# One routing step, token number times expert one-hot, read from constants in PSUM instead of from the one-hot in SBUF

## The chip, the cores and the metric

The program runs on one core of one Trainium2 chip. The metric is the device time of one execution in microseconds (us), lower is better. The core has five engines with instruction queues of their own: PE (matrix multiply), DVE (VectorE, elementwise and reductions), ACT (ScalarE), POOL (GpSimd) and SP (which issues most DMAs). Engines wait for one another on semaphores only; each runs its own queue strictly in order.

## What is computed

The reference is three layers, one after the other, on 768 tokens:

```python
attn_out = _attn_ref(**attn_kwargs)      # 8 heads, 64 wide, masked by hash bucket
x = attn_out.transpose(0, 2, 1, 3).reshape(B, S, H * D)     # 768 x 512
x = _moe_ref(x=x, **moe_kwargs)          # gMLP: w_in, gelu, spatial gate w_sg, w_out
return _moe2_ref(x=x, **moe2_kwargs)     # sticky top-1 mixture of 8 experts
...
for s in range(S):                       # in _moe2_ref
    fresh_e = int(np.argmax(logits[b, s]))
    e = fresh_e if s == 0 or local_gate[b, s] < 0.5 else prev_e
    prev_e = e
    h = np.maximum(x[b, s] @ w1[e], 0.0)
    out[b, s] = p[e] * (h @ w2[e])       # p: softmax of the logits
```

Every token goes to one expert: the one of its own highest logit, or, where its local gate says so, the one of the token ahead of it.

## The kernel before

The 768 tokens are six tiles of 128 (`t` = 0 to 5), a token to a partition. The program has four stretches: attention, the feed-forward part, mixing (spatial gate, output projection, residual, and the routing of each tile), and the eight experts. Every stretch is an order written out by hand: a text such as `MIXING` lists steps by name, and each engine's queue gets its instructions in the order in which the steps come. Nothing is reordered afterwards, so a step that waits holds all that stands behind it on its engine.

Weights of the experts stream in beside all this: step `wr` reads a quarter of a matrix (512 KB) into one of six raw buffers, `wh` casts it on ACT into the high half (L655), and `wl` subtracts the high half to get the low half, on DVE or POOL (L661). The low half is a 128 x 1024 subtraction with both sources in SBUF, and on POOL it runs for over 2 us.

In mixing, PE has four kinds of work, interleaved: `mix` (tile `vs`, L744, spatial gate), `out` (tile `o`, L767, output projection), small transposes and matmuls of the routing, and `gx` (L910, which gathers the tokens of an expert by a matmul with a selection matrix). DVE serves them: `gated` (tile `g`, L748) multiplies a finished `vs`, and PE transposes the product (`gT`, L754); `gl` (L759) splits it; `res` (L770) adds the residual.

The routing of one tile is the generator `route(t)`, and each word `route t` in `MIXING` runs it on to its next `yield`. Its steps are a chain through nearly all engines: transposes of x on PE (L781), logits on PE (tile `lg`, L791 to L799), the maximum on DVE (L802), the choice as a key per token (L819), a transpose of the key on PE into `route_bank` (L822), the running maximum over tokens (L824 to L839), which settles the expert of each token as a number `f` (L844), its one-hot `oh` (L846), ranks within the expert (L854), the selection matrix `pick` (L861), and the two parts of a small table, token number per expert (L868) and probability per expert (L872). The key of the next tile needs `carry` of this one.

`route_bank` is one bank of PSUM. Beside the transposed keys and the exponentials it holds two constants that were copied there once: `rev_p` (L924, eight numbers, one for each expert) and `iota_p` (L925). So L842, L846, L861 and L864 already read their tensor from PSUM. L868 is different: it reads `oh`, which L846 left in SBUF, multiplies by the token number `tok_1` (a scalar per partition) and writes eight numbers per token to `what_all` in SBUF.

Of the kernel before, what the change touches and what calls it, by code (L numbers as in the profile page):

```python
# [15 lines left out]
ALU = mybir.AluOpType  # L16
# [173 lines left out]
def kernel(  # L190
# [15 lines left out]
    nc = tc.nc  # L206
# [21 lines left out]
    tok_1 = sm[:, 32:38]  # L228
# [388 lines left out]
    what_all = cpool.tile([P, NT, 2, NE], F32, name="what_all")  # L617
# [49 lines left out]
    with ExitStack() as ctx_b:  # L667
# [109 lines left out]
        def route(t):  # L777
# [54 lines left out]
            f = bp2.tile([P, 1], F32, tag="rf", name="rf")  # L832
# [8 lines left out]
            oh = oh_all[:, t, :]  # L841
# [23 lines left out]
            yield "slot"  # L865
            nc.vector.tensor_scalar_add(se, se, 1e-9)
            yield "se"
            nc.vector.tensor_scalar(what_all[:, t, 0, :], oh, tok_1[:, t:t + 1], None, op0=ALU.mult)  # L868
            yield "id"
            nc.vector.reciprocal(se, se)  # L870
            yield "rse"
# [51 lines left out]
        rev_p, iota_p = route_bank[:, P:P + NE], route_bank[:, 2 * P:4 * P]  # L923
        nc.vector.tensor_copy(rev_p, revc)  # L924
        nc.scalar.copy(iota_p, iota2)  # L925
        routes = [route(t) for t in range(NT)]

        def side_b(name, t, k=0):
# [167 lines left out]
    with tc.If(n_extra > 0):  # L1096
        with ExitStack() as ctx_x:
# [13 lines left out]
            for t in range(NT):  # L1111
# [6 lines left out]
                                        op0=ALU.is_lt, op1=ALU.mult)  # L1118
                nc.vector.tensor_tensor(at[:, 0:1], at[:, 0:1], at[:, 1:2], op=ALU.add)
                nc.vector.scalar_tensor_tensor(ati, rank_all[:, t:t + 1], -float(P), at[:, 0:1],  # L1120
                                               op0=ALU.add, op1=ALU.add)
# [121 lines left out]
```

## Time and profile before

| | |
|---|---|
| median of 3 runs | 346.63 us (345.64 to 347.73) |
| the profiled execution | 347.04 us |
| its span, first to last instruction | 344.6 us |
| PE busy | 327.5 us (95%) |
| DVE busy | 272.5 us (79%) |
| ACT busy | 233.9 us (68%) |
| POOL busy | 203.5 us (59%) |
| mean granted PE clock | 0.989 of full speed |

Some 2.4 us of the profiled execution lie outside its span. Times within the trace are counted in us from the start of the span. A busy share says how full an engine was on average, not that it set the end: for that, the waits of each stretch and the chain of work that ended last are read. The ends of PE's instructions are modelled, because matmuls overlap in its pipeline; the starts are firmer.

### The profile page before, as it was taken

What the parts mean: (1) busy time and instruction counts of PE and PEld (TensorE: products, weight loads), DVE (VectorE), ACT (ScalarE), POOL (GpSimd) and SP (SyncE); (2) the same over time, 40 slices, a digit from 0 to 9 for tenths busy, and PEclk for the clock granted to TensorE, in tenths of its full rate; (3) what the DMA queues carried; (4) which work ended last, traced back from release to release, by engine and by line L of the source; (5) the groups of instructions that cost most, each with busy time, mean ns of one, the idle gap of its engine ahead of it and who ended that gap; (6) DMA issues with size and microseconds to landing.
All of it is one profiled execution on the core that took longest, in us unless ns stands there. A gap on an engine that the chain in (4) does not pass through costs nothing.

```text
span 344.6 us, 5450 instructions
## 1 busy us (share of the span) xinstructions
PE 327.5 (95%) x1860; PEld 256.8 (75%) x1860; DVE 272.5 (79%) x516; ACT 233.9 (68%) x432; POOL 203.5 (59%) x162
## 2 busy tenths in 40 slices
PE   7899999999999999999989999879999999999992
PEld 6787777667777657788767776559888888788892
DVE  4899999989998865788753768988589868798933
ACT  3589888888888775299455364364659786869540
POOL 3378867688858645247434674865732674574651
PEclk9999999999999999999999999998999999999997
DMA  6914043213421024011107429292979979999510
GB/s 248 331 45 153 3 152 121 92 38 119 133 82 61 10 62 132 0 57 52 46 7 253 124 89 327 81 357 66 343 252 303 336 288 368 348 330 364 216 60 32
DMA packets 25951, 55.82 MB, mean 162 GB/s; under 512 B 2878, under 2 KB 7486, under 8 KB 25920
## 3 DMA queue, kind: packets, MB, share of 16 engines
q1 hardware_dynamic: 23872, 50.67, 42.7%
q0 software_dynamic: 1120, 3.15, 2.7%
q10 hardware_dynamic: 928, 1.62, 1.4%
q8 instruction: 16, 0.26, 0.3%
q14 instruction: 15, 0.12, 0.1%
HBM read 52.28 MB, written 3.67 MB: 162 GB/s over the span
## 4 chain that ended last, share of the span: by engine, by line
PE 73%; DVE 13%; DMA 4%; ACT 4%; issue 2%; POOL 2%; SPq 0%; ACTq 0%; DVEq 0%; POOLq 0%
PE y L1045 10%; PE eh L1013 9%; PE t L437 9%; PE po L453 8%; PE s L420 5%; PE h L314 5%; PE s L423 5%; PE vs L744 5%; DMA raw<-in_w 3%; PE hv L314 3%; PE o L767 3%; PE pj L404 3%; PE gx L910 2%; PE hT L1024 1%; DVE what_all L868 1%
## 5 line engine op out<-in xcount | busy, mean ns | idle before, releaser
L661 POOL TENSOR_TENSOR w<-raw,w 128x1024 fp32r<-128x1024 f32 x23 | 58.6, 2549 | 40.3 <-ACT w L655 40.3
L655 ACT CAST w<-raw 128x1024 fp32r<-128x1024 f32 x64 | 65.3, 1052 | 12.7 <-DMA raw<-in_w 6.0
L661 DVE TENSOR_TENSOR w<-raw,w 128x1024 fp32r<-128x1024 f32 x41 | 59.9, 1492 | 5.1 <-ACT w L655 4.9
L443 ACT COPY pt<-t 128x384 f32<-128x384 f32 x96 | 43.4, 484 | 12.6 <-PE t L437 12.5
L431 ACT ACTIVATE e<-s,nb_all 128x768 f32<-128x768 f32 x48 | 43.6, 909 | 9.7 <-DVE nb_all L427 9.7
L427 DVE TENSOR_REDUCE nb_all<-s 128x1 f32<-128x768 f32 x48 | 45.4, 952 | 5.9 <-PE s L423 5.4
L437 PE MATMUL t<-ident,e 128*128 128x128 f32 x288 | 42.4, 274 | 0.0
L437 PEld LDWEIGHTS t<-ident,e 128*128 128x128 f32 x288 | 34.3, 140 | 8.6 <-ACT e L431 2.4
L453 PE MATMUL po<-pt,vt 128*64 128x384 f32 x192 | 35.4, 497 | 0.0
L1045 PE MATMUL y<-w,hh 128*128 128x512 f32 (+1 forms) x144 | 34.7, 374 | 0.3 <-ACT hh L1030 0.3
L420 PE MATMUL s<-k,q 128*128 128x384 f32 x96 | 28.5, 377 | 0.8 <-ACT e L431 0.7
L1045 PEld LDWEIGHTS y<-w,hh 128*128 128x128 f32 x144 | 24.4, 189 | 4.7 <-ACT hh L1030 0.8
L744 PE MATMUL vs<-vn,wshi 128*128 128x512 f32 x72 | 25.8, 406 | 1.4 <-ACT wshi L735 1.2
L423 PE MATMUL s<-k,q 76*128 76x384 f32 x96 | 25.1, 342 | 0.3 <-DVE q L411 0.3
L1013 PE MATMUL eh<-w,xh 128*128 128x512 f32 x96 | 25.0, 394 | 0.0
L392 POOL TENSOR_TENSOR k<-r,k 64x768 fp32r<-64x768 f32 x7 | 13.8, 1974 | 14.9 <-DVE k L382 9.5
L453 PEld LDWEIGHTS po<-pt,vt 128*64 128x64 f32 x192 | 12.0, 136 | 13.7 <-issue 13.4
L314 PE MATMUL h<-w_in_s,xTs 128*128 128x512 f32 x96 | 21.9, 389 | 0.0
L314 PEld LDWEIGHTS h<-w_in_s,xTs 128*128 128x128 f32 x96 | 18.0, 188 | 3.7
L1013 PEld LDWEIGHTS eh<-w,xh 128*128 128x128 f32 x96 | 17.7, 188 | 3.6
L420 PEld LDWEIGHTS s<-k,q 128*128 128x128 f32 x96 | 14.7, 190 | 7.2 <-ACT e L431 2.5
L1057 POOL DMA_INDIRECT out<-y,dst_row x8 | 12.3, 1532 | 11.2 <-ACT y L1054 4.7
(201 smaller groups left out, 738.4 us busy)
## 6 DMA issues: line engine op xcount, KB each, us to landing
raw<-in_w SPq DMA_DIRECT2D x64, 512.0 KB, 5.2
r<-in_qk SPq DMA_DIRECT2D x7, 768.0 KB, 4.4
raw<-in_w_in SPq DMA_DIRECT2D x8, 512.0 KB, 5.9
wsr<-in_w_sgT SPq DMA_DIRECT2D x6, 384.0 KB, 3.5
raw<-in_w_out SPq DMA_DIRECT2D x4, 512.0 KB, 3.5
vt<-in_v_tok ACTq DMA_DIRECT2D x1, 1536.0 KB, 9.3
xd<-x SPq DMA_DIRECT2D x6, 256.0 KB, 4.4
r<-in_qk SPq DMA_DIRECT2D x2, 384.0 KB, 4.0
```

The costliest lines, as they stand in the source:

```text
L314: nc.tensor.matmul(ps, a[:, kc, ts_], w_in_s[:, b, kc, ns], start=(kc == 0 and i == 0), stop=(kc == 3 and i == 2))
L420: nc.tensor.matmul(s[:, j, :HALF], q1[:, ts_], k1[:, j * HALF:(j + 1) * HALF], start=True, stop=False)
L427: nc.vector.tensor_reduce(nb_all[:, h, t:t + 1], ss[h, t][:, :, :HALF], axis=AX.XY, op=ALU.max, negate=True)
L431: nc.scalar.activation(e, ss.pop((h, t))[:, :, :HALF], AF.Exp, bias=nb_all[:, h, t:t + 1], accum_out=rs_all[:, h, t:t + 1])
L437: nc.tensor.transpose(ps[:, i * P:(i + 1) * P], es[h, t][:, g, i * P:(i + 1) * P], ident)
L443: nc.scalar.copy(dst, tps.pop((h, t, g))[:, :HALF].rearrange("p (i q) -> p i q", i=3))
L453: nc.tensor.matmul(po[j * D:(j + 1) * D, :HALF], vt[:, kt, h * D:(h + 1) * D], pt[j][:, kt, :], start=(kt == 0), stop=(kt == NT - 1))
L655: nc.scalar.copy(slabs_of[i, e][:, 0, q * 2:(q + 1) * 2, :], raws[part])
L661: eng.tensor_tensor(hl[:, 1, q * 2:(q + 1) * 2, :], raws.pop(part), hl[:, 0, q * 2:(q + 1) * 2, :].bitcast(F32), op=ALU.subtract)
L744: nc.tensor.matmul(ps, a[:, kc, :], b[:, kc, :], start=(k == 0), stop=(k == 17))
L1013: nc.tensor.matmul(ps[e, n], a[:, kc, :], slabs_of[1, e][:, b, kc * 2 + n, :], start=(k == 0), stop=(k == 11))
L1045: nc.tensor.matmul(yb[e][:, cs], a[:, kc, :], slabs_of[2, e][:, b, kc, cs], start=(k == 0), stop=(k == 23))
```

## The change

One instruction per tile is formed from other inputs. The one-hot is one where `rev_p` equals `f`; so the product of one-hot and token number can be formed in a single instruction from `rev_p` in PSUM and the two per-partition scalars `f` and `tok_1`, without reading `oh`:

```diff
@@ -865,7 +865,7 @@
             yield "slot"
             nc.vector.tensor_scalar_add(se, se, 1e-9)
             yield "se"
-            nc.vector.tensor_scalar(what_all[:, t, 0, :], oh, tok_1[:, t:t + 1], None, op0=ALU.mult)
+            nc.vector.tensor_scalar(what_all[:, t, 0, :], rev_p, f, tok_1[:, t:t + 1], op0=ALU.is_equal, op1=ALU.mult)
             yield "id"
             nc.vector.reciprocal(se, se)
             yield "rse"
```

The one-hot `oh` is still computed at L846, since L854 and L872 read it. On every engine the same instructions stand in the same places, with the same semaphores to wait for. This is DVE's queue around the step of tile 1, in mixing; `rf` is the scalar `f`, `sm` holds `tok_1`, and `se` is the sum of the softmax:

```order
 L864 TENSOR_SCALAR gbc<-route_bank,rank_all 128x128
 L866 TENSOR_SCALAR se<-se 128x1
-L868 TENSOR_SCALAR what_all<-oh_all,sm 128x8
+L868 TENSOR_SCALAR what_all<-route_bank,rf,sm 128x8
 L748 SCALAR_TENSOR_TENSOR g<-vs_2237,bsg,u_2_2030 128x512
 L759 SCALAR_TENSOR_TENSOR gl<-gT_2334,gh 128x512
```

Only the operands of the one instruction differ; the product `g` for PE's next transposes still stands right behind it. The other five places read alike.

## Rows read from the trace of the kernel before

**Rows 1.** The page's part 4, the chain that ended last, by line.

```profile
PE y L1045 10%; PE eh L1013 9%; PE t L437 9%; PE po L453 8%; PE s L420 5%; PE h L314 5%; PE s L423 5%; PE vs L744 5%; DMA raw<-in_w 3%; PE hv L314 3%; PE o L767 3%; PE pj L404 3%; PE gx L910 2%; PE hT L1024 1%; DVE what_all L868 1%
```

**Rows 2.** By stretch: us; busy PE, PEld, DVE, ACT, POOL; PEclk, DMA share, GB/s.

```profile
204.00:231.00 27.00, 22.45 (x150) 16.90 (x149) 23.36 (x93) 13.12 (x26) 17.85 (x9) 1.00 0.68 233
231.00:235.00 4.00, 3.98 (x20) 3.69 (x21) 2.48 (x14) 1.29 (x3) 4.00 (x4) 0.57 0.35 138
240.00:330.00 90.00, 89.67 (x442) 74.01 (x440) 75.27 (x70) 68.22 (x88) 50.66 (x24) 1.00 0.87 303
```

**Rows 3.** DVE's instructions by line: ns min/median/max, first and last start.

```profile
L868 DVE TENSOR_SCALAR what_all<-oh_all,sm x6: 221/1076/1906, 196.7 to 237.8; 128x8 f32<-128x8 f32 x6
...
L846 DVE TENSOR_SCALAR oh_all<-route_bank,rf x6: 216/226/227, 193.7 to 236.0; 128x8 f32<-128x8 f32 x6
...
L842 DVE TENSOR_SCALAR ohb_all<-route_bank,rf,pm x6: 276/277/285, 193.2 to 235.4; 128x8 bf16<-128x8 f32 x6
```

**Rows 4.** DVE's timeline: start, us, instruction, [idle before it <- releaser].

```profile
196.69 0.89 DVE L868 TENSOR_SCALAR what_all<-oh_all,sm 128x8 f32<-128x8 f32 x1
199.03 0.75 DVE L748 SCALAR_TENSOR_TENSOR g<-vs,bsg,u 128x512 f32<-128x512 f32 x1 [1.45 <-PE vs L744]
...
205.39 0.23 DVE L846 TENSOR_SCALAR oh_all<-route_bank,rf 128x8 f32<-128x8 f32 x1
...
207.03 1.91 DVE L868 TENSOR_SCALAR what_all<-oh_all,sm 128x8 f32<-128x8 f32 x1
...
217.85 1.56 DVE L868 TENSOR_SCALAR what_all<-oh_all,sm 128x8 f32<-128x8 f32 x1
...
219.92 0.15 DVE L802 TENSOR_REDUCE rmx<-lg 128x1 f32<-128x8 f32 x1
...
225.99 1.27 DVE L868 TENSOR_SCALAR what_all<-oh_all,sm 128x8 f32<-128x8 f32 x1
```

**Rows 5.** POOL's timeline, the four subtractions that L868 met.

```profile
195.14 2.40 POOL L661 TENSOR_TENSOR w<-raw,w 128x1024 fp32r<-128x1024 f32 x1
...
204.17 4.74 POOL L661 TENSOR_TENSOR w<-raw,w 128x1024 fp32r<-128x1024 f32 x2 [1.14 <-ACT w L655]
...
216.99 2.39 POOL L661 TENSOR_TENSOR w<-raw,w 128x1024 fp32r<-128x1024 f32 x1
...
224.86 2.37 POOL L661 TENSOR_TENSOR w<-raw,w 128x1024 fp32r<-128x1024 f32 x1 [1.90 <-ACT w L655]
```

**Rows 6.** PE's timeline around its three long waits for DVE.

```profile
207.02 0.39 PE L744 MATMUL vs<-vn,wslo 128*128 128x512 f32 x1
...
208.39 0.50 PE L744 MATMUL vs<-vn,wslo 128*128 128x512 f32 x1
209.65 0.66 PE L754 MATMUL gT<-ident,g 128*128 128x128 f32 x4 [0.76 <-DVE g L748]
...
218.47 0.29 PE L795 MATMUL lg<-cst,lts 128*128 128x9 f32 x2
...
219.40 0.63 PE L767 MATMUL o<-w_out_s,gh 128*128 128x512 f32 x2
221.49 0.29 PE L822 MATMUL route_bank<-ident,key 128*128 128x128 f32 x1 [1.47 <-DVE key L819]
...
228.74 0.30 PE L822 MATMUL route_bank<-ident,key 128*128 128x128 f32 x1 [1.57 <-DVE key L819]
```

**Rows 7.** PE's gx matmuls with x2h: busy us, mean ns; at 225:228, then 231:235.

```profile
L910 PE MATMUL gx<-pick,x2h 128*128 128x256 f32 x4 | 1.1, 299 | 0.0
...
L910 PE MATMUL gx<-pick,x2h 128*128 128x256 f32 x9 | 3.6, 405 | 0.0
```

**Rows 8.** Expert-weight subtractions by line: ns min/median/max, on DVE and on POOL.

```profile
L661 DVE TENSOR_TENSOR w<-raw,w x41: 1207/1218/3420, 181.4 to 328.8; 128x1024 fp32r<-128x1024 f32 x41
...
L661 POOL TENSOR_TENSOR w<-raw,w x23: 2370/2402/3347, 185.8 to 330.8; 128x1024 fp32r<-128x1024 f32 x23
```

## The prediction, made before the changed kernel ran

> **What bounds the kernel now.** I read the chain of work that ended last first. It is PE nearly throughout, but one line of DVE stands in it with 1% of the span: L868, the very instruction that is changed [rows 1]. An instruction of eight elements per partition has no business there, so the next view is its group by line: six executions, from 221 ns to 1,906 ns, with a median of 1,076 ns [rows 3]. Its sister L846, of the same size and also writing to SBUF, but reading from PSUM, never leaves 216 to 227 ns [rows 3]. Two of the six L868 ran in about 0.22 us; the other four took 0.89, 1.91, 1.56 and 1.27 us [rows 4].
>
> What stretches those four is seen by laying POOL's timeline beside DVE's. Each was issued while POOL ran a weight subtraction, and each ended just behind POOL's end: 197.58 against 197.54, 208.94 against 208.91, 219.41 against 219.38, 227.26 against 227.23 [rows 4, 5]. So the long duration is not work. L868, which reads and writes SBUF, is held until POOL is through. An instruction that reads its tensor from PSUM is not: L846 at 205.39 ran in 0.23 us in the middle of POOL's 204.17 to 208.91 [rows 4, 5].
>
> Then, who is late because of it? In 204 to 231 PE was busy for 22.45 of 27 us, so 4.55 us of PE stood empty there [rows 2]. In 240 to 330, the experts, it was busy for 89.67 of 90 us [rows 2]. Before and after this stretch PE has next to nothing to give; here it has, and its three long waits are all for DVE: 0.76 us for `g`, 1.47 and 1.57 us for a key [rows 6]. Each comes a little after one of the long L868 at 207.03, 217.85 and 225.99 [rows 4].
>
> **The change, part by part.** Nothing is added, removed or moved, on any queue; six instructions change one operand from SBUF to PSUM and get a second scalar.
>
> *Price of the new L868.* It is L846 with one more operation and one more scalar. L846 bounds it below (0.216 us); L842, which also reads `rev_p` and two scalars but writes another type, above (0.285 us) [rows 3]. I take 0.22 us, as L846 is nearer in output type. At the upper end, the three on the path would cost 0.2 us in all.
>
> One rule of the Trainium skill speaks against the change ("VectorE: DVE Perf Modes", in its section on the TRN2 errata): a Vector instruction pays a fixed 120 cycles with a source in PSUM against 58 with one in SBUF, at 0.96 GHz. By it, my estimate is some 0.065 us more for each instruction, 0.4 us for the six, and the change would lose wherever POOL is quiet. The rows do not bear this out at eight elements: 0.226 us from PSUM at the median against 0.221 us from SBUF when not held [rows 3]. So the sum goes without it.
>
> *Tile 0, L868 at 196.69.* It would be 0.67 us shorter. But DVE then sat idle for 1.45 us until PE had finished `vs` [rows 4]. That wait covers it: worth nothing, also if the cover shrank by half.
>
> *Tile 1, L868 at 207.03.* 1.91 becomes 0.22 us, and DVE is 1.69 us ahead. The next instruction, `g`, needs the `vs` whose last matmul runs on PE from 207.02 to 207.41 [rows 6], so it starts at about 207.45 and is still early enough. PE waited for it until 209.65, having been through with its last matmul at 208.89 by the modelled end, or free for the next one by about 208.7 by the pace of starts. So PE gains 0.76 to 0.95 us [rows 6]; I take 0.9. PE itself is late next.
>
> *Tile 2, L868 at 217.85.* 1.56 becomes 0.22 us, 1.34 us on DVE. The next maximum, at 219.92, needs the logits that PE finishes at 218.76 [rows 4, 6]; with 0.03 us for the semaphore it can come forward by 1.13 us at most. From there to the key all is in line on DVE and ACT, and PE's wait of 1.47 us is long enough to take all of that [rows 6]. Worth 1.13 us; 0.3 us of wait stay.
>
> *Tile 3, L868 at 225.99.* 1.27 becomes 0.22 us, 1.05 us on DVE. The logits behind it are there, the exponential follows the maximum, and PE's wait of 1.57 us for the key covers it [rows 6]. Worth 1.05 us; 0.5 us of wait stay.
>
> *Tiles 4 and 5.* Not held, 0.22 us before and after [rows 3]: nothing.
>
> *Sum:* 0.9 + 1.13 + 1.05 = 3.1 us by which PE, and all that it releases, reaches the experts earlier. The experts then run as a block: the weights come over buffers that are freed by the same engines, so they start earlier with it. DMA at 0.87 of its time in 240 to 330 is busy but not full [rows 2], and the time behind it is the same. On the profiled execution, 347.04 - 3.1 = 343.9 us. The median of the runs lies 0.41 us below that execution, which makes 343.5 us.
>
> *PE's clock, unknown.* In 231 to 235 the granted clock is 0.57 on average, so PE spent most of it at 1.2 GHz, the lower of its two levels; ahead of that, it had stood waiting for the key [rows 2, 6]. The nine `gx` matmuls with a high half there took 405 ns against 299 ns just before [rows 7]: 9 x 0.106 = 0.95 us, and as much again for those with the low half, which come one for one, 1.9 us in all. With shorter waits PE may keep 2.4 GHz. The bounds are 0 (it falls as before) and 1.9 us; if it does not fall I take 1.0, about the middle, since DVE's chain for tile 5, whose key PE transposes in that stretch, then becomes the bound for the rest. If it falls at another place, a stretch of the same length would cost about the same. In the sum I leave it as it was.
>
> **The rivals.** "Faster" and "slower" mean by more than 0.5%, 1.7 us; within that a measurement of this kernel can't tell it from no change.
>
> *B, the clock holds too.* As forecast, plus 1.0 us: 342.5. For it: the waits ahead of the fall shrink from 1.57 to 0.5 us and from 1.47 to 0.3 us. Against it: some 1.4 of the 4.55 us of idle time stay in the stretch ahead of it.
>
> *C, given back in the experts.* PE comes 3.1 us early, and the weight stream does not: a cast that waits for its DMA holds what stands behind it on ACT, and PE with it. For it: DMA raw stands in the chain with 3% [rows 1], some 10 us. Against it: the reads are released by subtractions that come earlier too. If half or more is lost, 345.0 to 346.6; I put it at 345.6.
>
> *D, the change doesn't do what it says.* L868 is still held, because it also writes to SBUF and reads its scalars there. L846 does both and is not held [rows 3, 4]. Time: 346.6. The Trainium skill ("SBUF — State Buffer", on the two sides of SBUF) has the shared port pair locked by a Vector instruction in a two-port mode or with two SBUF inputs, and held for a whole instruction. By that rule the scalars don't count and D falls; the four ends behind POOL's agree.
>
> *E, slower: the holds come back at L661.* DVE's own subtractions are held by POOL as well: 1,218 ns at the median, 3,420 ns at worst, so a hit costs up to 2.2 us [rows 8]. With DVE 3 us early against POOL the meetings fall anew in the experts, and DVE's queue holds the low halves that PE waits for. Two more hits on the path eat the gain and leave 346.63 - 3.1 + 4.4 = 347.9, within the bound; it decides from three on, 350.1 us. Against it: the meetings of today are as random, and PE stood idle there for only 0.33 us in 90 [rows 2].
>
> **How the numbers follow.** Forecast (A) 0.46: the holds are plain in the rows, and each wait that shrinks is named. B 0.30. C 0.13. D 0.05. E 0.06. A and B are faster: 0.76. C and D are the same: 0.18. E is slower: 0.06. The predicted time is A's, 343.5 us. The range reaches down past B to 341.4 (nearly the full 1.9 us for the clock, and a little scatter of the runs), and up to 345.6, which takes in a loss of two thirds of the gain; most of C, D and E stay outside, together some 0.2.
>
> **What would show it.** All six L868 at about 0.22 us, whatever POOL does. PE's wait for `g` gone, and those for the two keys down to 0.3 and 0.5 us; so PE's idle time in the stretch that was 204 to 231 falls from 4.55 to about 1.4 us. The first expert matmul comes 3.1 us earlier (4.1 in B, with no stretch at half clock). The forecast is wrong if L868 still ends with POOL's L661, if PE meets waits for other work at these places, or if PE's idle time in the experts grows from 0.3 us by as much as was won.

## The result, and the profile after

The changed kernel took 342.85 us, the median of 6 runs (342.15 to 343.22); the kernel before took 346.48 us, the median of 6 (345.55 to 347.73). The ratio is 0.9894, with a 95% interval of 0.9871 to 0.9918: 3.6 us, about 1.1%, faster. The profiled execution has a span of 340.8 us in place of 344.6.

The group of L868 by line in the profile after (ns min/median/max), beside [rows 3]:

```profile
L868 DVE TENSOR_SCALAR what_all<-route_bank,rf,sm x6: 275/276/279, 196.7 to 234.3; 128x8 f32<-128x8 f32 x6
```

The spread of 221 to 1,906 ns is gone. DVE's timeline after, beside [rows 4]:

```profile
207.06 0.28 DVE L868 TENSOR_SCALAR what_all<-route_bank,rf,sm 128x8 f32<-128x8 f32 x1
207.49 0.75 DVE L748 SCALAR_TENSOR_TENSOR g<-vs,bsg,u 128x512 f32<-128x512 f32 x1 [0.15 <-PE vs L744]
...
216.91 0.28 DVE L868 TENSOR_SCALAR what_all<-route_bank,rf,sm 128x8 f32<-128x8 f32 x1
217.87 0.17 DVE L802 TENSOR_REDUCE rmx<-lg 128x1 f32<-128x8 f32 x1
...
223.94 0.28 DVE L868 TENSOR_SCALAR what_all<-route_bank,rf,sm 128x8 f32<-128x8 f32 x1
```

POOL's timeline after, its subtractions at the same places, beside [rows 5]:

```profile
204.19 4.75 POOL L661 TENSOR_TENSOR w<-raw,w 128x1024 fp32r<-128x1024 f32 x2 [1.14 <-ACT w L655]
...
216.05 2.40 POOL L661 TENSOR_TENSOR w<-raw,w 128x1024 fp32r<-128x1024 f32 x1
...
222.82 2.37 POOL L661 TENSOR_TENSOR w<-raw,w 128x1024 fp32r<-128x1024 f32 x1 [0.79 <-ACT w L655]
```

POOL is as busy there as it was (17.89 us against 17.85), and all three L868 run in the middle of its subtractions, in 0.28 us. It is the meeting that became harmless; it didn't move away. PE's timeline after, at the three places of [rows 6], and its first expert matmul:

```profile
208.77 0.60 PE L754 MATMUL gT<-ident,g 128*128 128x128 f32 x4
...
219.45 0.29 PE L822 MATMUL route_bank<-ident,key 128*128 128x128 f32 x1 [0.35 <-DVE key L819]
...
225.71 0.29 PE L822 MATMUL route_bank<-ident,key 128*128 128x128 f32 x1 [0.59 <-DVE key L819]
...
235.51 3.83 PE L1013 MATMUL eh<-w,gxhi 128*128 128x512 f32 x16
```

The wait of 0.76 us is gone, and those of 1.47 and 1.57 us are 0.35 and 0.59 us. Busy time by stretch after, with the columns of [rows 2]:

```profile
204.00:228.00 24.00, 22.31 (x150) 16.98 (x149) 19.70 (x94) 13.15 (x26) 17.89 (x9) 1.00 0.72 244
...
228.00:231.00 3.00, 2.63 (x20) 2.23 (x20) 2.04 (x12) 1.30 (x3) 3.00 (x4) 1.00 0.84 330
231.00:235.00 4.00, 3.69 (x34) 3.31 (x33) 3.68 (x23) 1.39 (x3) 1.90 (x1) 1.00 0.24 31
...
236.00:326.00 90.00, 89.85 (x441) 74.31 (x440) 75.30 (x75) 68.87 (x89) 50.30 (x24) 1.00 0.86 304
```

The same 150 matmuls, in 24 us where they had 27, leave PE idle for 1.69 us, where it was 4.55. The granted clock stays at 1.00 in all these stretches; the half-speed stretch of [rows 2] is not there. And in 90 us of experts PE is idle for 0.15 us: nothing was given back.

### The profile page after: what moved, and what is told of

It reads as the page before. It is cut to its first block, busy times and chain, and to the rows that moved or that the text cites. A ratio compares the mean times of both kernels' runs of the same rounds, so it can differ in the third digit from the quotient of the medians.

```text
span 340.8 us, 5450 instructions
## 1 busy us (share of the span) xinstructions
PE 325.9 (96%) x1860; PEld 255.5 (75%) x1860; DVE 268.1 (79%) x516; ACT 234.4 (69%) x432; POOL 203.4 (60%) x162
## 4 chain that ended last, share of the span: by engine, by line
PE 74%; DVE 11%; ACT 5%; DMA 4%; issue 3%; POOL 2%; SPq 0%; ACTq 0%; POOLq 0%; DVEq 0%
PE eh L1013 9%; PE y L1045 9%; PE t L437 9%; PE po L453 9%; PE vs L744 6%; PE s L420 5%; PE h L314 5%; PE s L423 5%; PE o L767 4%; DMA raw<-in_w 3%; PE hv L314 3%; PE pj L404 3%; PE hT L1024 1%; DMA r<-in_qk 1%; ACT w L655 1%
```

## Experiments

All runs are compared with the kernel before. The executions scatter by some 2 us, so a second measure is read from each profile: the distance from the start of tile 0's L868, up to which nothing changes, to the start of the first expert matmul. In the kernel before it is 42.27 us (196.69 to 238.96), after 38.80 us. What follows the first expert matmul took 105.2 to 105.6 us in every profile.

| kernel | median us | ratio (95% interval) | distance us |
|---|---|---|---|
| the change | 342.85 | 0.9894 (0.9871 to 0.9918) | 38.80 |
| constants in SBUF | 346.22 | 0.9999 (0.9983 to 1.0014) | 42.41 |
| two tensors in SBUF | 346.81 | 1.0013 (0.9998 to 1.0027) | 42.22 |
| tiles 0, 4, 5 only | 346.60 | 1.0012 (0.9996 to 1.0028) | 42.83 |
| tile 1 only | 345.35 | 0.9974 (0.9959 to 0.9988) | 41.33 |
| tile 2 only | 345.40 | 0.9972 (0.9957 to 0.9987) | 41.06 |
| tile 3 only | 345.15 | 0.9958 (0.9941 to 0.9975) | 41.15 |
| all but tile 3 | 344.80 | 0.9947 (0.9923 to 0.9971) | 40.77 |
| before, PE's wait filled | 346.29 | 1.0006 (0.9989 to 1.0023) | 42.08 |
| the same, tile 4 in the new form | 345.84 | 0.9983 (0.9966 to 1.0001) | 42.26 |
| key first | 342.97 | 0.9901 (0.9872 to 0.9931) | 38.48 |
| key first, probability later | 342.08 | 0.9866 (0.9841 to 0.9891) | 37.65 |

The distances are of one execution each, and PE's clock differs among them, as told below.

**What holds L868?** The change does two things at once: the tensor comes from PSUM, and the one-hot is no longer needed. The first run keeps the new form and takes the constants from SBUF:

```diff
-nc.vector.tensor_scalar(what_all[:, t, 0, :], rev_p, f, tok_1[:, t:t + 1], op0=ALU.is_equal, op1=ALU.mult)
+nc.vector.tensor_scalar(what_all[:, t, 0, :], revc, f, tok_1[:, t:t + 1], op0=ALU.is_equal, op1=ALU.mult)
```

> The changed instruction as it is (is-equal to f, times the token number), but the eight constants are read from their copy in SBUF instead of PSUM. Theory (what counts is that the tensor lies in SBUF, and POOL holds such an instruction): L868 of tiles 0 to 3 ends with POOL's subtraction again, 0.9, 1.9, 1.5 and 1.2 us, the first expert matmul starts at about 239.0 us as before, time 346.5. Rival (the gain comes from the new form, which doesn't need the one-hot): 0.28 us each, first expert matmul at 235.5, time 342.9.

DVE's timeline of that run:

```profile
207.03 1.91 DVE L868 TENSOR_SCALAR what_all<-sm,rf 128x8 f32<-128x8 f32 x1
...
235.90 0.28 DVE L868 TENSOR_SCALAR what_all<-sm,rf 128x8 f32<-128x8 f32 x1
```

POOL's timeline of that run:

```profile
204.16 4.75 POOL L661 TENSOR_TENSOR w<-raw,w 128x1024 fp32r<-128x1024 f32 x2 [1.14 <-ACT w L655]
```

Held as before, to 208.94, with POOL through at 208.91, and nothing is gained in time (0.9999). For this instruction the form does nothing, the place of the tensor does all. The traces show no wait for POOL ahead of L868; it starts, and ends late. The opening says that engines wait for one another on semaphores only: this hold is an exception to it.

The unheld 0.28 us at tile 4 also prices the two parts of the new L868: with its tensor in SBUF it takes as long as with it in PSUM (0.276 us), and 0.06 us more than with one scalar. The new form has a second operation, too, but that is not what costs, as an instruction of the same size in the kernel before shows, with two operations and constants in place of both scalars:

```profile
L890 DVE TENSOR_SCALAR none<-table 128x8 f32<-128x8 f32 x1 | 0.2, 156 | 0.0
```

It reads PSUM and takes 0.156 us, against 0.226 us with one scalar and one operation (L846) and 0.277 us with two of each (L842). So it is each scalar read per partition that costs, some 0.06 us, and neither the operation nor PSUM.

The second run is the old product written with two tensors:

```diff
-nc.vector.tensor_scalar(what_all[:, t, 0, :], oh, tok_1[:, t:t + 1], None, op0=ALU.mult)
+nc.vector.tensor_tensor(what_all[:, t, 0, :], oh, tok_1[:, t:t + 1].to_broadcast([P, NE]), op=ALU.mult)
```

> L868 as a product of two tensors in SBUF, the one-hot and the token number broadcast over eight elements, in place of tensor times scalar. Theory (an instruction with two SBUF tensors is held by a POOL instruction that reads SBUF, too): four long ones as before, time 346.5. Rival (only an instruction of one SBUF source is held, since only that can use both read ports for it): about 0.23 us each, first expert matmul at 235.5, time 342.9.

DVE's timeline of that run, and POOL's one subtraction at tile 4:

```profile
206.94 1.90 DVE L868 TENSOR_TENSOR what_all<-oh_all,sm 128x8 f32<-128x8 f32 x1
...
235.44 0.44 DVE L868 TENSOR_TENSOR what_all<-oh_all,sm 128x8 f32<-128x8 f32 x1
237.60 0.16 DVE L868 TENSOR_TENSOR what_all<-oh_all,sm 128x8 f32<-128x8 f32 x1
...
233.50 2.37 POOL L661 TENSOR_TENSOR w<-raw,w 128x1024 fp32r<-128x1024 f32 x1
```

An instruction with two tensors in SBUF is held just as one with a single tensor is; at tile 4, where POOL ends at 235.87, it ends at 235.88. Left alone it takes 0.16 us. Its rival falls. The Trainium skill ("SBUF — State Buffer", on the two sides of SBUF) names two kinds of Vector instruction that meet POOL's lock, one in a two-port mode and one with two SBUF inputs. The holds seen here agree with it, though no trace tells in which mode an instruction ran.

Not every DVE instruction with its tensor in SBUF is held, though. Two others of the kernel before, L866 with one element per partition and L828 with a maximum over 128, and POOL's subtraction beside the second (the one beside the first is in [rows 5]):

```profile
206.97 0.14 DVE L866 TENSOR_SCALAR se<-se 128x1 f32<-128x1 f32 x1
...
213.55 0.29 DVE L828 TENSOR_REDUCE pm<-km 128x1 f32<-128x128 f32 x1
...
213.38 2.40 POOL L661 TENSOR_TENSOR w<-raw,w 128x1024 fp32r<-128x1024 f32 x1 [4.48 <-ACT w L655]
```

Both read and write SBUF, and both ran at once, in the middle of a subtraction. What sets them apart from L868 was not tested.

**Which tiles count?** The new form by a condition on `t`, the old form elsewhere:

```diff
+if t in (0, 4, 5):
     nc.vector.tensor_scalar(what_all[:, t, 0, :], rev_p, f, tok_1[:, t:t + 1], op0=ALU.is_equal, op1=ALU.mult)
+else:
+    nc.vector.tensor_scalar(what_all[:, t, 0, :], oh, tok_1[:, t:t + 1], None, op0=ALU.mult)
```

> The new form for tiles 0, 4 and 5 only. Theory: tile 0's hold is covered by DVE's wait for vs and tiles 4 and 5 are not held, so nothing: first expert matmul at 239.0, time 346.5 within 0.3. Rival (a hold of 0.67 us counts wherever it is): 0.6 us earlier.

Tile 0's L868 fell from 0.89 to 0.28 us and no time was won. The distance is even 0.56 us longer; in this execution the clock was at 0.50 in 231 to 235 and still at 0.84 in 235 to 239, where it was 0.57 and 1.00 before. In the next three runs the condition is `t in (1,)`, `(2,)` and `(3,)`:

> The new form for tile 1 only. Theory: PE's wait for g goes (0.76 us by the modelled ends, 0.9 by the starts), the two waits for keys stay at 1.5 and 1.6 us, the clock falls as before; first expert matmul at 238.1, time 345.6. Rival (the wait is paid at the next place, since DVE has its own chain): 346.5.

> The new form for tile 2 only. Theory: PE's first wait for a key falls from 1.47 to 0.3 or 0.4 us; the maximum behind it waits for the logits, so 1.1 of 1.3 us count; first expert matmul at 237.9, time 345.4. Rival: all of 1.3 us.

> The new form for tile 3 only. Theory: PE's second wait for a key falls from 1.57 to 0.6 us, 1.0 us: first expert matmul at 238.0 if the clock falls as before, at 237.6 if it stays at 1.00 because this was the wait that made it fall; time 345.5 or 345.1.

The distances are shorter by 0.94, 1.21 and 1.12 us, where 0.9, 1.13 and 1.05 were forecast; together 3.27, against 3.47 us for the whole change. By the medians beside them (346.16 us) the three gave 0.8, 0.8 and 1.0 us, together 2.6, against 3.6 us for the whole change. By either measure each tile's hold is a separate loss, paid at its own PE wait; by the medians the whole is 1.0 us more than its three parts. With tile 3 alone the clock stayed at 1.00 (the first row, columns as in [rows 2]), and something new shows in DVE's timeline (L871 is the old form there), beside POOL's:

```profile
231.00:235.00 4.00, 3.51 (x30) 3.01 (x30) 2.93 (x17) 1.29 (x3) 4.00 (x4) 1.00 0.63 244
...
235.25 0.61 DVE L871 TENSOR_SCALAR what_all<-oh_all,sm 128x8 f32<-128x8 f32 x1
...
233.46 2.37 POOL L661 TENSOR_TENSOR w<-raw,w 128x1024 fp32r<-128x1024 f32 x1
```

Tile 4's L868, not held before, has come early enough to run into POOL: it ends at 235.86, POOL at 235.83.

**What of the clock?** The opposite of the last run is the new form for all tiles but 3, `t in (0, 1, 2, 4, 5)`:

> The new form for all tiles but 3. Theory: 0.9 us from tile 1 and 1.1 us from tile 2, so PE's third wait, for the key of tile 4, stays at about 1.5 us; first expert matmul at 236.5 to 237.0, time 344.1 to 344.5. With that wait as long as before, the granted clock falls behind it as before (0.5 to 0.6 over some 3.5 us) if that wait is the cause; it stays at 1.00 if the two earlier waits were.

PE's waits for a key in 200 to 239 us of that run (us in all, times, longest), and its busy time by stretch, columns as in [rows 2]:

```profile
PE route_bank L822 <- DVE key L819: 2.0, 2, 1.6
...
226.00:228.00 2.00, 1.39 (x11) 1.42 (x12) 1.40 (x8) 2.00 (x5) 0.30 (x1) 0.87 1.02 355
228.00:235.00 7.00, 7.00 (x45) 6.81 (x44) 4.90 (x32) 1.81 (x4) 5.77 (x4) 0.55 0.33 128
```

The third wait stayed at 1.6 us, and the clock fell behind it, longer than before: a mean of 0.55 over 7 us is some 6 us at the lower level. So the distance shrank by 1.50 us only, half a microsecond less than forecast. The next run puts useless matmuls into that wait, in the kernel before (six, which the trace counts as twelve):

```diff
 pk = route_bank[:, :P]
+if t == 4:
+    for _ in range(6):
+        nc.tensor.matmul(gx[3][:, 2 * P:3 * P], ident, ident, start=False, stop=False)
```

> The kernel before, with six matmuls of 128 columns and no use put into PE's queue ahead of the transpose of tile 4's key, where PE stands waiting for 1.57 us. Theory (the clock fell because PE stood idle there): the granted clock stays at 1.00 in 231 to 235 us, the first expert matmul starts 0.4 to 1.0 us earlier than 239.0, time 345.5 to 346.1. Rival (the fall has another cause): 0.5 to 0.6 in that stretch as before, time 346.5.

Its rows: PE's timeline, the stretch behind it, tile 4's L868 (L871 there) and POOL's subtraction beside it:

```profile
226.92 1.50 PE L824 MATMUL gx<-ident 128*128 128x128 f32 x12
228.66 0.29 PE L825 MATMUL route_bank<-ident,key 128*128 128x128 f32 x1 [0.24 <-DVE key L819]
...
231.00:235.00 4.00, 3.53 (x30) 3.00 (x30) 2.93 (x18) 1.29 (x3) 4.00 (x4) 1.00 0.35 136
...
235.25 0.59 DVE L871 TENSOR_SCALAR what_all<-oh_all,sm 128x8 f32<-128x8 f32 x1
...
233.45 2.36 POOL L661 TENSOR_TENSOR w<-raw,w 128x1024 fp32r<-128x1024 f32 x1
```

With PE's wait filled the clock stayed at 1.00, and yet the time did not change (1.0006). Tile 4's L868 is held here as well, for 0.59 us. So the same filling was run with the new form for tile 4, `if t == 4`:

> The kernel before with PE's wait filled by six useless matmuls, which kept the clock at 1.00 and yet brought the first expert matmul only 0.19 us closer to tile 0's L868 (42.08 against 42.27 us), now with the new form for tile 4 as well. Theory (what the clock gave was mostly taken back, since tile 4's L868 then came early enough to be held by POOL for 0.59 us): L868 of tile 4 at 0.28 us, the distance at 41.6 to 41.8 us, time 345.8. Rival (DVE's chain of tile 5 is the bound there with or without that hold): 42.0 us and 346.2.

L868 of tile 4 took 0.28 us, but in the profiled execution the clock fell in spite of the filling:

```profile
231.00:235.00 4.00, 3.89 (x20) 3.69 (x20) 2.56 (x15) 1.30 (x3) 4.00 (x4) 0.60 0.36 142
```

So its distance says nothing, and one profile is not enough to tell what moves the clock. Every execution of an experiment, however, has its mean granted clock and its span on record. The five profiles in which the clock stayed at 1.00 there have means of 0.993 to 0.997, the eight in which it fell 0.986 to 0.991; so a mean of at least 0.993 is taken as a sign that it didn't fall. All 6 executions of the changed kernel have one. It was reached by none of 81 executions of the kernel before, by none of 34 with tile 1 alone, tile 2 alone, all but tile 3, or tiles 0, 4 and 5, and by one of ten in each of the first two experiments; but by 5 of 7 with tile 3 alone, 7 of 10 with the wait filled, and 8 of 10 with the filling and tile 4. What PE does in that one wait changes how likely the fall is, but doesn't settle it; nor is that wait the only thing that counts, as the two kernels below, in which it is shorter still or gone, reached such a mean in 3 of 6 executions each.

These executions also show a price: the 81 before have a mean span of 344.35 us; the 7 filled ones with the high clock 344.33; the 8 with tile 4 in the new form as well 343.64. A clock that doesn't fall is worth some 0.7 us, provided that the next L868 isn't held. That it is POOL's hold which takes the gain back otherwise fits these means and the one profile with the filling, but no run shows it by itself, and the ratio of the last run (0.9966 to 1.0001) doesn't quite exclude no change.

**The waits that stay.** In the changed kernel PE still waits 0.35 and 0.59 us for a key. In DVE's queue the probability of the tile before, L872, stands ahead of the key and waits there for ACT:

```profile
218.90 0.23 DVE L872 SCALAR_TENSOR_TENSOR what_all<-route_bank,se,oh_all 128x8 f32<-128x8 f32 x1 [0.41 <-ACT route_bank L815]
219.04 0.26 DVE L819 TENSOR_SCALAR key<-rw,sm,upd 128x1 f32<-128x1 f32 x1
```

Three words of `MIXING` were moved, with no change to any instruction (the lines are shown only around them):

```diff
-out 5 2, route 3, route 2, half 1 1, wl 0, half 2 1, route 3, res 4, route 3 *2,
+out 5 2, route 3, half 1 1, wl 0, half 2 1, route 3, res 4, route 2, route 3 *2,
...
-route 3, gx 1 0, route 4, wl 0, route 4, half 4 0,
+gx 1 0, route 4, route 3, wl 0, route 4, half 4 0,
...
-wh 0, route 4, route 5, route 4, route 5, wr 0, route 4, route 5, gx 0 2
+wh 0, route 4, route 5, route 4, route 4, route 5, wr 0, route 5, gx 0 2
```

> The changed kernel, with three steps of DVE's queue in another order: the probabilities of tiles 2 and 3 (L872) behind the key of the next tile in place of ahead of it, and the one-hot of tile 4 ahead of the exponential of tile 5. In the changed kernel L872 waits 0.41 and 0.35 us for ACT with the key behind it, and PE waits 0.35 and 0.59 us for that key. Theory: both waits of PE go or fall to 0.1, first expert matmul at 234.5 to 235.0 instead of 235.5, time 342.0 to 342.4. Rival (DVE's own chain through the routing is the bound and only its order changes): 342.9.

PE's timeline of that run:

```profile
219.29 0.32 PE L822 MATMUL route_bank<-ident,key 128*128 128x128 f32 x1 [0.50 <-DVE what_all L872]
```

The rival was nearer (342.97 us). The key was earlier, but its transpose writes into the bank that L872 reads, and L872 now stood between the two. One step further back, shown against that run:

```diff
-half 2 1, route 3, res 4, route 2, route 3 *2,
+half 2 1, route 3, res 4, route 3, route 2, route 3,
...
-gx 1 0, route 4, route 3, wl 0, route 4, half 4 0,
+gx 1 0, route 4, wl 0, route 4, route 3, half 4 0,
```

> As in the kernel with the key first, but L872 of tiles 2 and 3 one step further back, behind the product km, which itself waits for PE's transpose of the key. There L872 had moved into PE's way: the transpose into the same PSUM bank waited for it (0.8 us in two waits), and first expert matmul less tile 0's L868 was 38.48 us against 38.80 us in the changed kernel. Theory: PE's two waits fall below 0.3 us each, that distance to 38.0 to 38.3 us, time 342.2 to 342.6. Rival (the transpose waits for ACT's exponential in the same bank just as long): 38.5 us and 342.9.

All waits of PE in 200 to 239 us of that run, in us, times, longest:

```profile
PE x2T L781 <- DVE x L770: 0.4, 1, 0.4
PE table L880 <- ACT route_bank L815: 0.4, 1, 0.4
PE rk L851 <- DVE ohb_all L842: 0.3, 1, 0.3
PE rk L851 <- DVE se L866: 0.3, 1, 0.3
```

The waits for keys are gone, the distance is 37.65 us, and the time 342.08 us, at a ratio of 0.9866 (0.9841 to 0.9891). By the distance that is 1.15 us better than the change alone, by the medians 0.8 us; but the two intervals overlap, and the two kernels were compared with the kernel before, not with each other.

## Why the prediction was right

It said 343.5 us (341.4 to 345.6), and 342.85 was measured. It went out from 346.63 us, the median of three runs; by the six runs beside the change the kernel before takes 346.48, so the gain was 3.6 us where 3.1 was forecast. Point by point:

- *The hold.* Shown, by the run with the constants in SBUF, which differs from the change in nothing but the place of the tensor. Rival D, that it stays held, fell.
- *The price of the new L868.* Mis-sized: 0.22 us was taken, 0.276 measured, near the upper bound of 0.285. I chose by the type of the output; the number of scalars counted. It cost under 0.2 us on the path, as bounded. The rule of the Trainium skill that a source in PSUM costs more ("VectorE: DVE Perf Modes", in its section on the TRN2 errata) didn't show at eight elements: 0.28 us from either memory.
- *Tile 0, worth nothing.* Shown, with tiles 4 and 5, by a ratio of 1.0012 (0.9996 to 1.0028).
- *Tiles 1, 2 and 3: 0.9, 1.13 and 1.05 us.* Measured alone: 0.94, 1.21 and 1.12 by the distance, 0.8, 0.8 and 1.0 by the medians. The place of each also held: `g` waits 0.15 us for `vs` now, and the two waits for keys kept 0.35 and 0.59 us of the forecast 0.3 and 0.5. PE's idle time in the stretch fell to 1.69 us, where some 1.4 was forecast.
- *PE's clock.* This is the term that was mis-sized. The sum left it as it was, with B as second case at 1.0 us. B's condition held in the profile after, and by their mean clocks in all six executions; what it is worth is some 0.7 us where it could be isolated. The whole change gained 0.2 us more than its three tiles by the distance and 1.0 us more by the medians, and the clock's share is in that; its size in the changed kernel is not known better. So the result lies between A and B, and that it came so near to A is in part luck: by the medians the three tiles gave 2.6 us, half a microsecond less than the sum has for them, and the clock, which the sum left out, made up for it.
- *The experts run as a block.* Shown: the distance is 3.47 us shorter, the span 3.8, and PE's idle time in the 90 us of experts went from 0.33 to 0.15 us. Rivals C and E fell. E's mechanism, an instruction that comes earlier and meets POOL anew, is real, but in another place: tile 4's L868 was held anew when it came earlier in the old form. The change had put that one out of reach, too; in the profile after it meets POOL and takes 0.28 us:

```profile
232.30 0.28 DVE L868 TENSOR_SCALAR what_all<-route_bank,rf,sm 128x8 f32<-128x8 f32 x1
...
230.51 2.39 POOL L661 TENSOR_TENSOR w<-raw,w 128x1024 fp32r<-128x1024 f32 x1
```

What remains open is what exactly makes the clock fall: with the same filled wait it fell in some executions and not in others. Open is also why L866 and L828, with their tensors in SBUF, are not held.

## What to carry to other kernels

When a short DVE instruction shows a wide spread of durations, lay POOL's timeline beside it before counting it as work: ends that fall together point to a hold, and a run with the tensor in the other memory shows it. Reading the tensor from PSUM takes such an instruction out of POOL's way at no price that could be measured at this size, and it pays only where the wait ends on the engine that sets the time: three of four holds did here. An instruction made early runs into whatever POOL does then, so all copies of such an instruction are to be changed, also those that are not held today; and in a queue that runs in order, what waits for another engine belongs behind what other engines wait for.

## What was not expected

Two tensors in SBUF are held as one is (1.90 us against 1.91), although the instruction is otherwise the shortest of the forms tried, 0.16 us. Each scalar read per partition costs some 0.06 us, the memory of the tensor nothing at this size. And the same kernel, with PE's wait filled, had its clock fall in some executions and not in others, so one profile can't price the clock.
